# One planned kernel, a new plan: instruction fetches and a slow first clock window booked, sigmoid ordered later, some copies and one scaling in four on VectorE, new urgencies

## The chip, the core and the metric

The kernel runs on one core of a Trainium2 chip. Its metric is the device time in microseconds (us), as the median of several runs. A run's time is that of the whole execution; a profiled execution also has a span, from the first to the last instruction. The engines are PE (TensorE, the matrix engine, with PEld for its weight loads), DVE (VectorE), ACT (ScalarE), POOL (GpSimd) and SP (SyncE, which here only issues DMAs).

## The reference, cut to what matters

The input has 2048 rows of 640 channels, all in float32.

```python
def _A_ref(q, k, v, shift_k, ssm_k, ssm_D):
    k_shift = jnp.zeros_like(k)                     # causal depthwise convolution with 4 taps
    for t in range(ks):
        k_shift = k_shift + k_pad[:, t:t + S, :] * shift_k[:, ks - 1 - t][None, None, :]
    kv = k_shift * v
    y_f = rfft(kv padded to 2S) * rfft(ssm_k padded to 2S)   # per channel
    y = irfft(y_f)[:S] + kv * ssm_D                 # long causal convolution and a skip
    return q * y

def _B_ref(x, w1, b1, w2, b2):
    h = jnp.einsum("bsd,df->bsf", x, w1) + b1
    h = relu(h) ** 2
    return jnp.einsum("bsf,fd->bsd", h, w2) + b2

sa, ca, ga, sb, cb, gb = split(_silu(c) @ w_mod, 6)
h = _layernorm(x) * (1 + ca) + sa                   # x is A_q
x = x + ga * _A_ref(h, A_k, A_v, A_shift_k, A_ssm_k, A_ssm_D)
h = _layernorm(x) * (1 + cb) + sb
x = x + gb * _B_ref(h, B_w1, B_b1, B_w2, B_b2)
```

## The kernel before, in words

**Recording and planning.** The kernel's code does not issue instructions. Each helper adds a node to a graph: an engine, a cost, the tiles it reads and writes, and a key with a number within that key. `Graph.order` (L225) then plans: it runs through a modelled time, and whenever an engine is free it gives it the ready node with the highest urgency for which a buffer is free. The urgency comes from the table `URGE` (L1277; a key's list, one number per node, in tenths), and from the length of the work behind a node where the table has no entry. `emit` (L432) issues all nodes in the planned order, and `keep_order` (L525) pins each engine to that order. So costs and rules of the planner act on the chip only through the order in which each engine's instructions stand, and through the buffers that are given to tiles. All instructions that are issued this way have L439 in the profile (SP's DMAs L632), so they are told apart by tile names.

**What the planner books.** For PE it books the work of a group, an entry and leaving time when the shape of the array's use changes from group to group (`ENTER`, `LEAVE`, L30-31; 64x64, 64x128, 128x128 and so on), a slower clock in windows of 3.4 us after windows with little PE work (`rate`, L229), and one fetch of instructions for every 256 PE instructions (L375-379). DVE instructions with two inputs in SBUF, and all POOL instructions, are booked as exclusive of each other (`lock`). SP has at most six DMAs in flight (`OUT`, L26; the waits are real ones, L631-636), and a DMA may be issued 2 us before its urgency (`HOLD`, `early`, L308).

**First part: the convolution, for 5 blocks of 128 channels.** Per block b: `kv_load` and `kv` (L840, L849) load k and v (tiles named KV), transpose them on PE (`ident,KV`), do the four taps on ACT, DVE and POOL (tiles kacc or KV, with ktail and kover for the three columns that cross a tile's edge), multiply by v, and store the product in DRAM (`kv_d`). `load_h` and `load_x` (L897, L902) load the long filter (`in_A_ssm_k`) and that product into the tile `p`, 4 DMAs each; behind each filter DMA POOL adds the skip `dsm` to the first column (`p<-p,dsm`). `unit_a` (L919) is the first Fourier stage: per block 4 units on the filter and 4 on the product, each of 32 matmuls of 64x64 on PE (`cst,p`), which the trace shows as 64 records, since it shows a float32 matmul twice (and a transpose once). `spectra` (`a,gb`) is the second stage; `front` multiplies the two spectra on DVE and combines them on POOL (tiles wx); `back` (`gi,wx`) and `unit_y` (`ident,q`, then `wx,cst` and `we,cst`) go back to time. In `unit_y` a copy from PSUM to SBUF stands behind each transposition, two per unit (L1026, keys `tc`). `prep` (L1063) normalizes q with four scalings of 128x128 on ACT (L1071, `KV<-xp,nm,rs` and `up<-xp,nm,rs` in the trace), multiplies by a row on DVE and adds a row on POOL; `finish` adds the result to q and stores it (`x_d`). `awake` (L907) adds 20 groups of four transpositions of the unit matrix that nobody reads, to keep PE's clock up; they are booked to the key `warm` and go where the planner puts them.

**Beside it:** `q_stats` takes the statistics of q on DVE, `mod_start` (L740) loads c and takes its sigmoid on ACT, `mod_row` and `mod_col` scale rows of w_mod on ACT by silu(c), add them on POOL (tiles wm) and sum them on PE (`wm,ones`), which gives the rows that `prep` needs. The weights of the MLP are split into two parts on ACT, DVE and POOL (tiles w_S, w_W, w_KA).

**Second part: the MLP, for 8 chunks of 256 rows.** `prep_hat` normalizes, `prep_xt` transposes and splits into two parts (tiles mtmp, xfs, xt), `mlp_front`, `mlp_middle`, `mlp_back` and `mlp_out` follow, with PE matmuls of `xt,w` and of `w,hring`. The table has no entry for most of this part.

Of the kernel before, what the change touches and what calls it, by code (L numbers as in the profile page):

```python
# [13 lines left out]
AF = mybir.ActivationFunctionType  # L14
# [17 lines left out]
ALIKE = 2.0  # L32
ENTER = {(64, 128): 0.104}
# [88 lines left out]
class Graph:  # L122
# [102 lines left out]
    def order(self, lag=0.06, pelag=0.1, phase=0.0):  # L225
# [82 lines left out]
        def early(n):  # L308
            return 1e4 if not n.told else HOLD if n.engine == "SP" else 30.0 if n.key[0] == "warm" else 1e4
# [14 lines left out]
        block, ent = 0.0, 0  # L324
# [6 lines left out]
        while done < len(nodes):  # L331
            moved = False
            for e in ready:
                while free[e] <= t + 1e-9:
# [30 lines left out]
                    if e == "PE":  # L365
# [4 lines left out]
                        last = end = run(t, work)  # L370
# [130 lines left out]
def ssm_mlp_kernel(  # L501
# [153 lines left out]
    def cost(engine, op, args, kw):  # L655
# [7 lines left out]
        if engine == "DVE":  # L663
# [351 lines left out]
    def unit_y(b, l):  # L1015
        ts = []
        qv = QT[b].rearrange("p (n c) k -> p n (c k)", c=2)
        for h in range(2):
# [7 lines left out]
            copy(dve if b == NB - 1 and h else act, s, t)  # L1026
# [36 lines left out]
    def prep(b, j):  # L1063
# [190 lines left out]
    def mlp_out(n):  # L1254
# [18 lines left out]
        if n < NC - 1:  # L1273
# [4 lines left out]
        ("b1", 0): [-1644, -1479],  # L1278
        ("comb", 0): [-476, -465, -479, -469, -486, -532, -539, -490, -546, -553, -560, -582, -600, -614, -607, -640,
            -647, -657, -664],  # L1280
        ("comb", 1): [-952, -962, -966, -945, -995, -955, -988, -1006, -1000, -1024, -1013, -1031, -1053, -1118,
            -1098, -1111, -1105, -1195, -1208],
        ("comb", 2): [-1509, -1547, -1533, -1512, -1551, -1540, -1526, -1561, -1554, -1591, -1590, -1625, -1618,
            -1697, -1690, -1757, -1720, -1767, -1750],
        ("comb", 3): [-1958, -1954, -1937, -1969, -1989, -1982, -1975, -2006, -1999, -2013, -2085, -2066, -2092,
            -2163, -2099, -2157, -2146, -2190, -2183],
        ("comb", 4): [-2392, -2385, -2396, -2403, -2436, -2410, -2429, -2495, -2440, -2476, -2354, -2509, -2502,
# [440 lines left out]
```

## Time and profile before

| | |
|---|---|
| median of 3 runs | 702.28 us (702.1 to 705.56) |
| the profiled execution's own time | 701.26 us |
| its span | 699.5 us |
| what lies around the span | 1.76 us |
| mean granted PE clock | 0.982 |
| PE busy | 653.8 us (93% of the span) |
| DVE, ACT, POOL busy | 398.8, 328.1, 261.4 us |

Times in the trace are counted from the span's start. A row of the timeline has start, length, engine, operation, output and inputs, and in square brackets how long the engine was idle before it and what ended that wait. "issue" means that nothing the profile shows was waited for. In the groups by line, the numbers behind the bar are the busy time in us, the mean length of one instruction in ns, and the idle time before them.

### The profile page before, as it was taken

What the parts mean: (1) busy time and instruction counts of PE and PEld (TensorE: products, weight loads), DVE (VectorE), ACT (ScalarE), POOL (GpSimd) and SP (SyncE); (2) the same over time, 40 slices, a digit from 0 to 9 for tenths busy, and PEclk for the clock granted to TensorE, in tenths of its full rate; (3) what the DMA queues carried; (4) which work ended last, traced back from release to release, by engine and by line L of the source; (5) the groups of instructions that cost most, each with busy time, mean ns of one, the idle gap of its engine ahead of it and who ended that gap; (6) DMA issues with size and microseconds to landing.
All of it is one profiled execution on the core that took longest, in us unless ns stands there. A gap on an engine that the chain in (4) does not pass through costs nothing.

```text
span 699.5 us, 17953 instructions
## 1 busy us (share of the span) xinstructions
PE 653.8 (93%) x7593; PEld 588.6 (84%) x7593; DVE 398.8 (57%) x782; ACT 328.1 (47%) x678; POOL 261.4 (37%) x332
## 2 busy tenths in 40 slices
PE   8859889789889999799999999999999999999996
PEld 8748669658778878499989889999999999999996
DVE  2855846879569367867345474375355463563532
ACT  3626666897777775556323253224233243242220
POOL 2607539969749477444101321004013021030000
PEclk9899999999999999999999999999999999999999
DMA  9797899898954856224002010020020020110011
GB/s 233 211 265 249 220 247 204 246 225 180 244 124 128 169 165 182 87 76 142 0 9 68 19 58 1 1 75 1 1 76 1 9 68 1 30 47 1 1 39 37
DMA packets 108292, 72.42 MB, mean 104 GB/s; under 512 B 48498, under 2 KB 95666, under 8 KB 108212
## 3 DMA queue, kind: packets, MB, share of 16 engines
q1 hardware_dynamic: 106304, 70.80, 39.2%
q8 instruction: 59, 0.97, 0.6%
q10 hardware_dynamic: 1844, 0.48, 0.4%
q14 instruction: 21, 0.17, 0.1%
q0 software_dynamic: 64, 0.01, 0.0%
HBM read 56.85 MB, written 14.42 MB: 102 GB/s over the span
## 4 chain that ended last, share of the span: by engine, by line
PE 83%; DVE 6%; issue 4%; POOL 3%; ACT 2%; DMA 1%; DVEq 0%; SPq 0%; ACTq 0%; POOLq 0%
PE ps L439 83%; DVE KV L439 2%; DMA wm<-in_w_mod_dram 1%; DVE mtmp L439 1%; POOL kover L439 1%; POOL KV L439 1%; ACT a L439 1%; DVE x L439 1%; DVE xt L439 0%; ACT KV L439 0%; DVE up L439 0%; POOL xt L439 0%; ACT wm L439 0%; POOL wm L439 0%; DVE wx L439 0%
## 5 line engine op out<-in xcount | busy, mean ns | idle before, releaser
L439 PE MATMUL ps<-xt,w_S 128*128 128x512 f32 (+1 forms) x935 | 176.8, 332 | 5.4 <-DVE xt L439 2.4
L439 PEld LDWEIGHTS ps<-xt,w_S 128*128 128x128 f32 x935 | 142.2, 190 | 20.4 <-DVE xt L439 2.6
L439 PE MATMUL ps<-w_S,hring 128*128 128x320 f32 x648 | 109.5, 310 | 0.0
L439 ACT ACTIVATE mtmp<-ps,b1t 128x256 f32<-128x256 f32 (+1 forms) x112 | 51.4, 473 | 110.9 <-PE ps L439 102.8
L439 PEld LDWEIGHTS ps<-w_S,hring 128*128 128x128 f32 x648 | 99.0, 188 | 2.1 <-DVE mtmp L439 0.2
L439 DVE TENSOR_TENSOR mtmp<-ps,mtmp 128x256 f32<-128x256 f32 (+1 forms) x99 | 41.0, 420 | 76.8 <-ACT mtmp L439 76.0
L439 PE MATMUL ps<-a,gb 128*64 128x128 f32 x1260 | 80.7, 286 | 1.8 <-ACT a L439 1.0
L439 PEld LDWEIGHTS ps<-a,gb 128*64 128x64 f32 x1260 | 75.0, 144 | 8.0 <-ACT a L439 3.2
L439 DVE TENSOR_TENSOR hring<-mtmp,hring 128x256 fp32r<-128x256 f32 x74 | 39.0, 532 | 50.8 <-ACT hring L439 50.5
L439 PEld LDWEIGHTS ps<-cst,p 64*64 64x64 f32 x2560 | 43.8, 141 | 25.9 <-issue 18.2
L439 PE MATMUL ps<-cst,p 64*64 64x64 f32 x2560 | 49.1, 228 | 17.5 <-issue 12.8
L439 ACT ACTIVATE hring<-mtmp 128x256 fp32r<-128x256 f32 x74 | 30.6, 415 | 73.4 <-PE ps L439 60.0
L439 POOL TENSOR_TENSOR wx<-wx 128x256 f32<-128x256 f32 x80 | 60.0, 771 | 3.9 <-DVE wx L439 3.4
L439 POOL TENSOR_TENSOR x<-x,gb2row 128x640 f32<-128x640 f32 x16 | 25.7, 1625 | 92.0 <-ACT mtmp L439 92.0
L439 POOL TENSOR_TENSOR x<-mtmp,x 128x640 f32<-128x640 f32 (+1 forms) x9 | 13.1, 1461 | 121.9 <-DVE mtmp L439 121.9
L439 ACT ACTIVATE a<-ps 128x512 f32<-128x512 f32 x72 | 41.2, 635 | 35.8 <-PE ps L439 35.7
L439 PE MATMUL ps<-w_S,w_W 128*128 128x320 f32 x312 | 52.7, 308 | 0.0
L439 DVE TENSOR_TENSOR wx<-ps,wx 128x512 f32<-128x512 f32 x64 | 41.2, 685 | 14.9 <-PE ps L439 10.4
L439 PEld LDWEIGHTS ps<-w_S,w_W 128*128 128x128 f32 x312 | 48.3, 188 | 1.2
L439 DVE SCALAR_TENSOR_TENSOR mtmp<-mtmp 128x256 f32<-128x256 f32 x91 | 44.5, 497 | 1.9
L439 PE MATMUL ps<-gi,wx 64*128 64x128 f32 x640 | 40.8, 278 | 3.0 <-issue 1.8
L439 PEld LDWEIGHTS ps<-gi,wx 64*128 64x128 f32 x640 | 37.2, 188 | 6.8 <-issue 4.6
(140 smaller groups left out, 1067.7 us busy)
## 6 DMA issues: line engine op xcount, KB each, us to landing
wm<-in_w_mod_dram SPq DMA_DIRECT2D x25, 320.0 KB, 5.2
KV<-in_A_k_dram SPq DMA_DIRECT2D x20, 256.0 KB, 5.7
p<-in_A_ssm_k_dram SPq DMA_DIRECT2D x20, 256.0 KB, 5.6
KV<-in_A_v_dram SPq DMA_DIRECT2D x20, 256.0 KB, 5.2
p<-kv_d SPq DMA_DIRECT2D x20, 256.0 KB, 5.2
xp<-in_A_q_dram SPq DMA_DIRECT2D x10, 512.0 KB, 8.3
q<-in_A_q_dram SPq DMA_DIRECT2D x7, 640.0 KB, 5.7
out_dram<-x SPq DMA_DIRECT2D x14, 320.0 KB, 3.6
```

The source lines that it names most:

```text
L439: fn(*real, **{k: a.real() if isinstance(a, View) else a for k, a in kw.items()})
```

## The change

Nothing is added to or taken from the computation. There are six edits:

1. The planner books PE's fetches in another way: the first 63 entries of a block of 256 count as already used, a fetch takes 3.6 us, or 5.5 us where a modelled transfer is under way, and a group waits only when PE gets to the next block before its fetch is done.
2. PE's first clock window of 3.4 us is booked as slow.
3. The DMAs that store the output are no longer held back until 2 us before their urgency.
4. The sigmoid is ordered behind the last store of `kv_d` of block 0 in the plan (not by a wait on the chip).
5. In `unit_y` the second copy of each unit is on DVE for blocks 2, 3 and 4 (before: for block 4 only): 8 copies of 128x512 move from ACT to DVE. In `prep` the fourth scaling of each group is a `tensor_scalar` on DVE: 20 of 80 scalings move, and a cost for such an instruction with an input in PSUM is added.
6. All urgencies are other numbers.

```diff
+FETCH = (3.6, 5.5)
@@ rate
                 if k < 4:
-                    slow[k] = False
+                    slow[k] = k == 0
@@ early
-            return 1e4 if not n.told else HOLD if n.engine == "SP" else 30.0 if n.key[0] == "warm" else 1e4
+            return 1e4 if not n.told else HOLD if n.engine == "SP" and n.key[0] != "out" else 30.0 if n.key[0] == "warm" else 1e4
@@ order
-        block, ent = 0.0, 0
+        block, ent = 0.0, 63
...
-                        last = end = run(t, work)
+                        end = run(t, work)
+                        ent += n.entries
+                        if ent >= 256:
+                            ent -= 256
+                            at = end - (end - t) * ent / n.entries
+                            block, late = max(at, block), max(0.0, block - at)
+                            end += late
+                            block += FETCH[dma_free > block]
+                        last = end
...
-                    if e == "PE":
-                        ent += n.entries
-                        if ent >= 256:
-                            end = max(end, block + 4.0)
-                            block, ent = end, ent - 256
@@ cost
+            if op == "tensor_scalar" and deep and len(ins) > 2:
+                return 0.28 + 0.001 * n
@@ mod_start
         act.activation(sg, ct, AF.Sigmoid)
+        g.nodes[-1].deps.add(max(n.id for n in g.nodes if n.key == ("kst", 0)))
@@ unit_y
-            copy(dve if b == NB - 1 and h else act, s, t)
+            copy(dve if b > 1 and h else act, s, t)
@@ prep
-            act.activation(u[:, i], XPt[b][:, l], AF.Identity, scale=rs, bias=nm)
+            if i == 3:
+                dve.tensor_scalar(u[:, i], XPt[b][:, l], rs, nm, op0=ALU.mult, op1=ALU.add)
+            else:
+                act.activation(u[:, i], XPt[b][:, l], AF.Identity, scale=rs, bias=nm)
@@ URGE
-        ("b1", 0): [-1644, -1479],
...
```

The table moves almost every instruction of the first part. Three places show how.

**SP, from the program's first DMA on** (KV are tiles of k and v, `p_0` is block 0's tile for filter and product, `gb` a table of the second Fourier stage, `q_8` rows for the statistics). Before:

```order
L632 DMA KV_87<-in_A_k_dram 128x4x128
L632 DMA p_0_107<-in_A_ssm_k_dram 128x8x64
L632 DMA KV_87<-in_A_v_dram 128x4x128
L632 DMA p_0_107<-in_A_ssm_k_dram 128x8x64
L632 DMA KV_87<-in_A_k_dram 128x4x128
L632 DMA KV_87<-in_A_v_dram 128x4x128
L632 DMA KV_87<-in_A_k_dram 128x4x128
L632 DMA p_0_107<-in_A_ssm_k_dram 128x8x64
L632 DMA KV_87<-in_A_v_dram 128x4x128 x2
L632 DMA KV_87<-in_A_k_dram 128x4x128
L632 DMA gb_270<-in_gb_dram 128x1024
L632 DMA p_0_107<-in_A_ssm_k_dram 128x8x64
```

Of the change:

```order
L637 DMA p_0_106<-in_A_ssm_k_dram 128x8x64
L637 DMA KV_87<-in_A_k_dram 128x4x128
L637 DMA p_0_106<-in_A_ssm_k_dram 128x8x64
L637 DMA KV_87<-in_A_k_dram 128x4x128
L637 DMA p_0_106<-in_A_ssm_k_dram 128x8x64
L637 DMA KV_87<-in_A_v_dram 128x4x128 x2
L637 DMA p_0_106<-in_A_ssm_k_dram 128x8x64
L637 DMA KV_87<-in_A_v_dram 128x4x128
L637 DMA KV_87<-in_A_k_dram 128x4x128
L637 DMA q_8_247<-in_A_q_dram 128x1280
L637 DMA KV_87<-in_A_k_dram 128x4x128
L637 DMA gb_332<-in_gb_dram 128x1024
```

The fourth filter tile moves from the 13th to the 8th DMA; statistics rows come ahead of the last k tile and of gb. On PE, at the same place, 13 of the 20 groups of `awake` now stand ahead of the first unit (before: all 20); the other seven stand singly further on.

**PE, around the last units on block 1's product** (`cst,p_1` is such a unit, `wm_1_0,ones` sums a row of w_mod, `we,cst` and `wx,cst` belong to `unit_y`). Before, two whole units stand on each side of one half of the row's sum:

```order
L439 MATMUL ps3_93<-cst_76,p_1_457 64x64 x2
L439 MATMUL ps2_92<-cst_76,p_1_457 64x64 x2
L439 MATMUL ps3_93<-cst_76,p_1_457 64x64 x2
L439 MATMUL ps6_96<-wm_1_0_1055,ones_70 128x320
L439 MATMUL ps0_90<-cst_76,p_1_457 64x64 x2
L439 MATMUL ps1_91<-cst_76,p_1_457 64x64 x2
L439 MATMUL ps0_90<-cst_76,p_1_457 64x64 x2
```

Of the change, with the sum elsewhere:

```order
L444 MATMUL ps2_92<-cst_76,p_1_390 64x64 x2
L444 MATMUL ps3_93<-cst_76,p_1_390 64x64 x2
L444 MATMUL ps7_97<-we_89,cst_76 64x512
L444 MATMUL ps7_97<-wx_88,cst_76 64x512
L444 MATMUL ps6_96<-ident_63,KV_87 128x128 x4
L444 MATMUL ps5_95<-ident_63,q_0_1070 128x128 x4
L444 MATMUL ps4_94<-ident_63,KV_87 128x128 x4
L444 MATMUL ps2_92<-cst_76,p_1_390 64x64 x2
L444 MATMUL ps3_93<-cst_76,p_1_390 64x64 x2
```

The four units (128 program matmuls) now stand in pieces of 32, 48, 16 and 32 with transpositions and `unit_y` matmuls between them. Counted over the whole PE order, the shape of the array's use changes 120 times before and 132 times in the change; 5 of the 12 more are around single groups of `awake`.

**POOL, where the MLP begins** (`x1_0` and `x1_1` are the first two chunks, `gb2row` a row that is added to them, `xp_4` and `up0` are block 4's results). Before:

```order
L439 TENSOR_TENSOR gb2row_3877<-gb2row_3877,gbrow_4023 128x640
L439 TENSOR_TENSOR xp_4_3352<-xp_4_3352,up0_1190 128x512 x2
L439 TENSOR_TENSOR x1_0_2083<-x1_0_2083,gb2row_3877 128x640
L439 TENSOR_TENSOR xp_4_3352<-xp_4_3352,up0_1190 128x512
L439 TENSOR_TENSOR x1_0_2083<-x1_0_2083,gb2row_3877 128x640
L439 TENSOR_TENSOR mtmp_4075<-mtmp_4075 128x256 x3
```

Of the change:

```order
L444 TENSOR_TENSOR gb2row_3962<-gb2row_3962,gbrow_3977 128x640
L444 TENSOR_TENSOR xp_4_3334<-xp_4_3334,up0_1222 128x512 x2
L444 TENSOR_TENSOR x1_0_2026<-x1_0_2026,gb2row_3962 128x640 x2
L444 TENSOR_TENSOR x1_1_2085<-x1_1_2085,gb2row_3962 128x640
L444 TENSOR_TENSOR xp_4_3334<-xp_4_3334,up0_1222 128x512
L444 TENSOR_TENSOR x1_1_2085<-x1_1_2085,gb2row_3962 128x640
```

The last `xp_4` addition moves out from between the two `x1_0` additions to behind the first `x1_1` addition.

More of the change, by code (lines that the diff above doesn't have):

```diff
@@ new lines, in ssm_mlp_kernel @@
+        ("gate", 0): [-2578, -2550, -2477, -2522, -2586, -2553, -2441, -2518, -2541, -2525, -2665, -2544, -2066,
+            -2040, -2191, -2162, -2757, -2610, -2653, -3144, -3160, -3208, -3035, -2775],
+        ("gb", 0): [-208, -235, -311, -280],
+        ("gi", 0): [-1270, -1263, -1315, -1211],
+        ("h", 1): [-534, -692, -519, -1139, -904, -1044, -1021, -964, -971, -393, -988, -1022, -1044, -1327, -742,
+            -1186],
+        ("h", 2): [-411, -1382, -1398, -1399, -3243, -1563, -1764, -1583, -1533, -1610, -1373, -1635, -1627, -1665,
+            -527, -1705],
@@ new lines, in ssm_mlp_kernel @@
+        ("h", 3): [-554, -1801, -1606, -1808, -3035, -1979, -2203, -1997, -434, -2025, -2182, -1940, -4250, -2115,
+            -1405, -1900],
+        ("h", 4): [-3332, -2315, -2437, -2413, -1874, -2467, -230, -1809, 1621, -2229, -90, -2601, -228, -2405, -250,
+            -3098],
+        ("hat", 0): [-2382, -2788],
+        ("hat", 1): [-2811, -2839],
[25 rows of a table added]
+        ("kst", 0): [-296, 584, -47, -332],
+        ("kst", 1): [987, -567, 1035, 204],
+        ("kst", 2): [-1046, -1140, -1284, -1242],
+        ("kst", 3): [-1282, -1424, -1000, -1147],
@@ new lines, in ssm_mlp_kernel @@
+        ("kst", 4): [-1347, -1835, -1314, -1716],
+        ("kt", 0): [-297, -620, 1686, 124],
+        ("kt", 1): [-72, -491, 1344, -767],
+        ("kt", 2): [-1378, -955, -1274, -1261],
+        ("kt", 3): [-1339, -1370, -1464, -1769],
+        ("kt", 4): [-1503, -2322, -1652, -1379],
+        ("lgb", 0): [-176, -246],
+        ("lgi", 0): [-476, -55, -499],
[35 rows of a table added]
+        ("lxp", 0): [-1077, -764],
+        ("lxp", 1): [-1171, -984],
+        ("lxp", 2): [-1508, -1583],
+        ("lxp", 3): [-1455, 249],
@@ new lines, in ssm_mlp_kernel @@
+        ("mul", 2): [-1540, -1533, -1569, -1548, -1573, -1580, -1590, -1597, -1639, -1760, -1654, -1661, -1717,
+            -1724, -1763, -1756],
+        ("mul", 3): [-1998, -2007, -2014, -2034, -2055, -2041, -2083, -2070, -2090, -2097, -2135, -2128, -2188,
+            -2181, -2196, -2203],
+        ("mul", 4): [-2436, -2437, -2452, -2445, -2470, -2463, -2488, -2481, -2505, -2498, -2542, -2535, -2560,
+            -2554, -2600, -2584],
+        ("out", 0): [-3379, -3410, -3372, -3434, -3425, -3460, -3999, -3991],
[8 rows of a table added]
@@ new lines, in ssm_mlp_kernel @@
+        ("pac", 4): [-2226, -2252, -2258, -2260, -2195, -2203, -2220, -2232, -2423, -2424, -2336, -2342, -2374,
+            -2408, -2396, -2414],
+        ("pra", 0): [-1272, -1160, -1189, -1155, -1174, -1190, -1159, -1152, -687, -1174, -1165, -1133, -1143, -990,
+            -1139, -1128],
+        ("pra", 1): [-1295, -1301, -1278, -1335, -1498, -1528, -1525, -1395, -1420, -1395, -1426, -1384, -1524,
+            -1469, -1301, -1263],
+        ("pra", 2): [-1732, -1958, -1766, -1699, -1716, -1720, -1688, -1686, -1674, -1666, -1672, -1660, -1681,
+            -1625, -1688, -1664],
@@ new lines, in ssm_mlp_kernel @@
+        ("pra", 3): [-2143, -2093, -2085, -2098, -2085, -2132, -2130, -2137, -2103, -2112, -1846, -2114, -2073,
+            -2108, -2119, -2117],
+        ("pra", 4): [-2295, -2327, -2313, -2295, -2301, -2435, -2361, -2292, -2383, -2332, -2369, -2298, -2321,
+            -2357, -2342, -2289],
+        ("prm", 0): [-1315, -1308, -1183, -1158],
+        ("prm", 1): [-1325, -1702, -1435, -1631],
+        ("prm", 2): [-1816, -1740, -1692, -1709],
+        ("prm", 3): [-2255, -2222, -2174, -2215],
@@ new lines, in ssm_mlp_kernel @@
+        ("prm", 4): [-2352, -2425, -2392, -2385],
+        ("prp", 0): [-1418, -1332, -1203, -1190],
+        ("prp", 1): [-1470, -1761, -1498, -1844],
+        ("prp", 2): [-1884, -1944, -1904, -1821],
+        ("prp", 3): [-2350, -2337, -2274, -2281],
+        ("prp", 4): [-2362, -2557, -2375, -2342],
+        ("qp", 0): [-216, -1009, 984, 193],
+        ("qp", 1): [-1094, -1153, -1193, -1267],
+        ("qp", 2): [-992, -1499, -1629, -1918],
+        ("qp", 3): [-1336, -1708, -1168, -795],
+        ("qp", 4): [-2334, -2216, -2218, -2043],
```

129 lines of the change are left out of this document (33 added, 96 removed), and 356 rows, old and new, of the table URGE.

## The prediction

> **What bounds the kernel now.** I read first the page's chain of work that ended last, then the busy time in two windows, cut where the MLP's matmuls begin.
>
> ```profile
> PE 83%; DVE 6%; issue 4%; POOL 3%; ACT 2%; DMA 1%; DVEq 0%; SPq 0%; ACTq 0%; POOLq 0%
> ...
> 0.00:291.00 291.00, 257.23 (x5026) 215.83 (x5026) 190.65 (x325) 193.57 (x372) 180.29 (x251) 0.96 0.80 201
> 291.00:699.50 408.50, 396.56 (x2568) 372.78 (x2567) 208.12 (x458) 134.55 (x306) 81.11 (x82) 0.99 0.12 34
> ```
>
> The columns of a window are its length, busy time (and count) of PE, PEld, DVE, ACT and POOL, granted clock, DMA share and GB/s. PE is the bound, and its work is unchanged. So a new order can only win back PE's idle time: 33.8 us before 291 us, and 11.9 us after it, of which the end of the program takes a part that no order removes. Next, who ended PE's waits, and the queue that carries instructions:
>
> ```profile
> PE ps L439 <- issue: 15.0, 11, 4.0
> ...
> q8 instruction: 59, 0.97, 0.6%
> ```
>
> Nearly half of the early idle time, 15.0 us in 11 waits, waits for nothing that is computed. The queue moved 0.97 MB in 59 packets, 16.4 KB each; PE's 7593 matmuls and as many weight loads make 64 bytes per instruction, so one packet is 257 instructions, or 128 matmuls. The chain in order of time shows that spacing:
>
> ```profile
> 96.56 1.73 issue
> ...
> 230.25 0.67 issue
> 230.92 7.16 PE ps L439 x127
> 238.09 0.26 issue
> 238.35 4.66 PE ps L439 x128
> 243.01 0.32 issue
> 243.33 3.25 PE ps L439 x127
> 246.58 0.85 issue
> ```
>
> Each "issue" wait stands 127 or 128 matmuls behind the last. PE waits when it runs through a block faster than the next is fetched; from wait's end to wait's end is 7.4, 5.0 and 4.1 us. These are the lengths of a fetch here, with other transfers under way in the first and few in the last.
>
> **Term 1, fetches: -1.7 us.** To price a block in the new order I use the mean cost per record of four groups:
>
> ```profile
> L439 PE MATMUL ps<-cst,p 64*64 64x64 f32 x2560 | 49.1, 228 | 17.5 <-issue 12.8 <-POOL p L439 4.3 <-ACT a L439 0.4
> L439 PE MATMUL ps<-a,gb 128*64 128x128 f32 x1260 | 80.7, 286 | 1.8 <-ACT a L439 1.0 <-DVE KV L439 0.8
> L439 PE MATMUL ps<-ident,KV 128*128 128x128 f32 x160 | 24.3, 288 | 3.5 <-DVE KV L439 1.6 <-DVE a L439 0.8 <-DMA KV<-in_A_k_dram 0.4
> ...
> L439 PE MATMUL ps<-wx,cst 128*64 128x512 f32 x40 | 21.3, 614 | 0.0
> ```
>
> They give 0.019, 0.064, 0.152 and 0.53 us (the last for a pair: `we,cst` writes the other 64 partitions beside `wx,cst`). A block of only `cst,p` records runs 2.5 us, shorter than any fetch above. Counted along both orders, the block that ends in the 1.73 us wait at 96.56 ran about 3.2 us by these costs; its successor holds 12 transpositions and four `unit_y` pairs beside 108 records of units, 1.8 + 2.1 + 2.1 = 6.0. That wait goes: -1.7. Of the waits from 230 to 247 (2.1 us together) the two shortest blocks grow from about 4.4 and 3.5 us to 5.4 and 4.7, above the fetches of 5.0 and 4.1; 0.6 us may stay at the long fetch: -1.5. Against that, one block of block 2's filter units shrinks from 5.7 to 3.9, and one of block 4's from 4.4 to 3.2: at a fetch of 4.1 to 5.0 they add about 1.0 and 0.5. The three short blocks of block 0's product units stay (8.4 us of work before, 8.8 now). Bounds: with other work covering the new short blocks -3.2; with a fetch of 7.4 us at both, +4.5.
>
> The Trainium skill, "Runtime: NRT & Kernel Launch", section "Instruction fetch mechanics", says that the sequencer fetches 16 KiB blocks of 256 instructions and that crossing a boundary is "mostly hidden". The block size agrees with 16.4 KB per packet; "hidden" does not agree with 15.0 us here. By that rule this term would be 0, and the sum below 1.7 us higher.
>
> **Term 2, the start: -2.5 us.**
>
> ```profile
> 1.35 10.62 PE L439 MATMUL ps<-ident 128*128 128x128 f32 x80 [1.35 <-POOL ident masks.py:199]
> ...
> 23.39 2.08 PE L439 MATMUL ps<-cst,p 64*64 64x64 f32 x64 [2.51 <-POOL p L439]
> ...
> 8.11 0.37 POOL L439 TENSOR_TENSOR p<-p,dsm 128x8 f32<-128x8 f32 x2
> ```
>
> PE spends 10.62 us on 80 `awake` transpositions, though the first two filter tiles are ready at 8.48 (POOL's row). With 52 of them the units start at about 8.5, 3.4 us sooner, and the moved 28 fill later waits. The fourth filter tile, behind which PE waits 2.51 us before 23.39, goes out as the 8th DMA instead of the 13th. What is late next is the gb table, which now stands behind 640 KB more, and the stores of the kv product. Bounds: 0 if those end the stage as now, -3.4 if nothing does. I take three quarters.
>
> **Term 3, changes of shape: +1.0 us.**
>
> ```profile
> 50.77 0.69 PE L439 MATMUL ps<-cst,p 64*64 64x64 f32 x32 [1.44 <-issue]
> 51.39 0.65 PE L439 MATMUL ps<-ident,KV 128*128 128x128 f32 x4
> ...
> 58.80 1.16 PE L439 MATMUL ps<-cst,p 64*64 64x64 f32 x64
> 59.89 2.84 PE L439 MATMUL ps<-a,gb 128*64 128x128 f32 x48
> ```
>
> From start to next start, 32 records take 0.62 us and 64 take 1.09: 0.0147 each and 0.15 per visit. Twelve more changes cost 1.8 us; the five around single `awake` groups I put into waits, which leaves 1.0. Bounds 0 and 1.8.
>
> **Term 4, work from ACT to DVE: 0.**
>
> ```profile
> 70.00:105.00 35.00, 30.10 (x480) 22.02 (x480) 22.75 (x52) 24.22 (x43) 15.94 (x21) 0.95 0.89 233
> 105.00:140.00 35.00, 31.37 (x638) 27.77 (x634) 25.48 (x40) 26.22 (x55) 31.97 (x46) 1.00 1.01 225
> 140.00:175.00 35.00, 31.21 (x581) 24.84 (x580) 29.61 (x47) 28.41 (x61) 28.17 (x35) 1.00 0.85 202
> ...
> L439 ACT ACTIVATE KV<-xp,nm,rs 128x128 f32<-128x128 f32 x56 | 24.5, 492 | 1.7 <-DVE up L439 1.4 <-POOL xp L439 0.3
> ...
> L439 ACT ACTIVATE wx<-ps 128x512 f32<-128x512 f32 x49 | 29.2, 597 | 15.2 <-PE ps L439 12.9 <-ACT KV L439 1.1 <-ACT up L439 0.8
> ...
> L439 DVE COPY hs<-ps 128x512 f32<-128x512 f32 x4 | 2.7, 686 | 1.3 <-PE ps L439 1.3
> ...
> L439 DVE TENSOR_SCALAR mtmp<-x,rs,nm 128x640 f32<-128x640 f32 x1 | 0.6, 614 | 0.0
> ...
> L439 DVE TENSOR_SCALAR cbs<-ps 128x5 f32<-128x5 f32 x2 | 0.3, 160 | 5.5 <-PE ps L439 5.5
> ```
>
> ACT loses 20 x 0.492 and 8 x 0.597, 14.6 us. DVE gains 8 x 0.686 and 20 scalings of 128x128, which lie between 0.160 (five columns) and 0.614 us (640); I take 0.25, on the straight line between the two: 10.5 us in all, at most 17.8. Two in five scalings belong to blocks 0 and 1, whose stage is 105 to 175 us. There DVE has 55.1 us of 70 busy, ACT 54.6: 2.0 more on DVE fit its gaps, as 3.9 less on ACT opens its own. Bounds -2 and +7 (the rival below).
>
> **Term 5, the MLP's begin: -1.0 us.**
>
> ```profile
> 289.86 1.55 POOL L439 TENSOR_TENSOR x<-x,gb2row 128x640 f32<-128x640 f32 x1 [1.11 <-ACT mtmp L439]
> ...
> 291.37 1.27 POOL L439 TENSOR_TENSOR xp<-xp,up 128x512 f32<-128x512 f32 x1
> 291.46 3.13 DVE L439 TENSOR_TENSOR xt<-xfs,xt 128x256 fp32r<-128x256 f32 x2 [0.46 <-ACT xt L439]
> ...
> 292.60 1.72 POOL L439 TENSOR_TENSOR x<-x,gb2row 128x640 f32<-128x640 f32 x1
> ...
> 294.65 0.57 PE L439 MATMUL ps<-xt,w_S 128*128 128x256 f32 x2 [2.35 <-DVE xt L439]
> ```
>
> Two DVE subtractions with both inputs in SBUF take 3.13 us while POOL adds without a gap until 294.32, and PE waits 2.35 us for them. The order moves the 1.27 us `xp` addition out of that run, so it can end 1.3 sooner, and a bit is lost to the addition that now follows. Bounds -2.4 and +1.
>
> **Term 6, other waits from 70 to 175 us: -1.0.** PE is idle 12.3 us in the three windows above, 10.6 without the 1.73 us fetch, in waits that the fetches do not explain. The new order has the statistics and the w_mod rows earlier, with other waits in their place that the old trace cannot show; I take a tenth off, bounds -4 and +4.
>
> **The sigmoid: 0.** Its table load moves from a time at which ACT had nothing to do to one at which it has little:
>
> ```profile
> 6.24 1.28 ACT L439 ACT_TABLE_LOAD   x1 [1.98 <-DMA cst<-in_cw_dram]
> ...
> 40.00:50.00 10.00, 5.13 (x192) 4.67 (x192) 4.19 (x9) 1.64 (x3) 0.21 (x1) 0.83 1.02 317
> ```
>
> ACT's 8.4 free us there cover it; without them it costs 1.3. Releasing output stores earlier changes nothing while the MLP's stores have no urgencies in the table: 0.
>
> **Sum.** -1.7 - 2.5 + 1.0 - 1.0 - 1.0 = -5.2 us against the profiled execution's 701.26 us, of which 1.76 lie around the span: 696.1. The median of the runs shown is 1.0 above that execution, so I forecast 697.1 us. The measurement of this kernel tells about 0.5% (3.5 us) from no change: faster is below 698.8, slower above 705.8.
>
> **Rivals.** *DVE becomes the bound from 105 to 175 us, slower (chance 0.27).* DVE instructions that use SBUF wait for POOL additions there, as at 291.46, and POOL has 60.1 of 70 us busy. If each of the 8 moved scalings waits for one whole addition (1.27 us) and takes its upper price (0.61), DVE gets 15.0 us, just its 14.9 us of gaps, and most of it would delay the taps and with them PE: +10 to the sum, 707 us. It decides from about half of the scalings waiting. For it: the page's chain runs through DVE and POOL rows in that stage. Against: ACT, the other link, gets freer, and 12 scalings lie later, where PE lost almost nothing to DVE. The Trainium skill, "SBUF — State Buffer", section "Who interferes with whom", states that `tensor_scalar` can take a mode that locks a port pair shared with GpSimd for the whole instruction; the 3.13 us row agrees for subtraction, and no run here shows it for a scaling.
>
> *The early gain is swallowed, no change (0.22).* DMA has 0.89, 1.01 and 0.85 of its time busy in the three windows of term 4. If transfers end each of these stages, terms 2 and 6 are 0: 701.26 - 1.7 + 1.0 - 1.0, plus 1.0, is 700.6 us.
>
> *The fetch booking does not do what it says (0.05).* If fetches on the chip don't follow blocks as booked, term 1 is 0: 698.8 us.
>
> *Far more goes (0.10).* If the plan also removes most of term 6's 10.6 us, 688 us.
>
> **How the numbers follow.** The forecast has 0.36. Faster: 0.36 and 0.10, and half of the 0.05: 0.48. Same: 0.22 and the rest, 0.25. Slower: 0.27. The range reaches over forecast, swallowed gain and the nearer half of the DVE rival: 690 to 707.5 us. The case of faster alone has 693 to 699.
>
> **What would show it.** Term 1: "issue" waits of about 12 to 13 us instead of 15.0, and no such wait among block 1's last units. Term 2: the first `cst,p` record at 8.5 instead of 11.9 us, and no wait for POOL p near 23. Term 3: `cst,p` busy time up by about 1 us. Term 4: scalings on DVE of about 0.25 us; the rival, if they last over 1 us. Term 5: the wait for DVE xt under 1.5 us. The forecast is wrong if PE's idle time before the MLP stays above 32 us.

## The result, and the profile after the change

The changed kernel takes 696.72 us (median of 20 runs, 692.48 to 701.29), the kernel before 702.32 us (median of 20, 697.04 to 710.1). The ratio is 0.9929, 95% interval 0.9905 to 0.9953: faster, by 0.5 to 0.95%. The forecast was 697.1. Its sum was right, half of its terms were not; that their errors cancel was luck.

The profiled execution of the changed kernel took 697.55 us, span 695.7: 3.7 us less than the profiled one of before, where the medians differ by 5.6. First its page's chain and two windows, cut as before just ahead of the MLP's first matmul (now at 287.60):

```profile
PE 83%; DVE 5%; ACT 4%; DMA 3%; issue 3%; POOL 1%; SPq 0%; DVEq 0%; ACTq 0%; POOLq 0%
```

```profile
0.00:286.80 286.80, 255.28 (x5026) 214.13 (x5026) 203.83 (x357) 177.53 (x339) 181.15 (x251) 0.98 0.76 200
286.80:695.70 408.90, 397.62 (x2568) 374.38 (x2567) 205.19 (x455) 137.33 (x311) 80.81 (x82) 0.99 0.13 37
```

PE's idle time before the MLP is 31.5 us instead of 33.8. That is 2.3 us of the gain; PE's busy time is also less, 255.3 instead of 257.2 us, for the same matmuls at a granted clock of 0.98 instead of 0.96. After the cut the time is 0.4 us longer. The largest of PE's waits in the whole profile, grouped by who ended them (total, times, longest; the one for `xt` is the MLP's):

```profile
PE ps L444 <- issue: 12.0, 9, 2.7
PE ps L444 <- ACT a L444: 6.6, 7, 2.4
PE ps L444 <- DVE wx L444: 3.0, 5, 1.2
PE ps L444 <- DVE xt L444: 2.6, 1, 2.6
```

Issue waits fell from 15.0 to 12.0 us. All other waits until the MLP's first matmul rose a little, from 19.2 to 19.9 us; the largest share now waits for ACT's `a`. So in this pair of profiles the gain of 3.8 us of span is 3.0 from fetches and 1.9 of busy time, which goes with the higher clock, less 0.7 in other waits and 0.4 after the MLP began. The timeline of the waits that the steps below speak of:

```profile
9.73 2.10 PE L444 MATMUL ps<-cst,p 64*64 64x64 f32 x128
...
22.92 2.08 PE L444 MATMUL ps<-ident,KV 128*128 128x128 f32 x12 [2.51 <-ACT kacc L444]
...
43.00 5.04 PE L444 MATMUL ps<-cst,p 64*64 64x64 f32 x224 [2.38 <-ACT a L444]
49.90 0.68 PE L444 MATMUL ps<-cst,p 64*64 64x64 f32 x28 [1.86 <-issue]
...
178.17 0.44 PE L444 MATMUL ps<-cst,p 64*64 64x64 f32 x10 [1.80 <-issue]
...
227.84 0.48 PE L444 MATMUL ps<-gi,wx 64*128 64x128 f32 x2 [2.74 <-issue]
```

The units begin at 9.73 instead of 11.90, the long wait for POOL p at 23.39 is gone, and one of the same length for ACT kacc stands at 22.92. No issue wait is left among block 1's last units (94 to 98 us); a new one of 2.74 us stands in block 4.

### The profile page after: what moved, and what is told of

Same layout as the page of the kernel before. It is cut to its first block, busy times and chain, and to the rows that moved or that the text cites. A ratio compares the mean times of both kernels' runs of the same rounds, so it can differ in the third digit from the quotient of the medians.

```text
span 695.7 us, 17972 instructions
## 1 busy us (share of the span) xinstructions
PE 652.9 (94%) x7593; PEld 588.5 (85%) x7593; DVE 409.0 (59%) x810; ACT 314.9 (45%) x650; POOL 262.0 (38%) x332
## 4 chain that ended last, share of the span: by engine, by line
PE 83%; DVE 5%; ACT 4%; DMA 3%; issue 3%; POOL 1%; SPq 0%; DVEq 0%; ACTq 0%; POOLq 0%
PE ps L444 83%; DVE KV L444 2%; ACT a L444 2%; DVE wx L444 1%; DMA p<-in_A_ssm_k_dram 1%; DVE mtmp L444 1%; DMA kv_d<-KV 1%; DMA p<-kv_d 1%; DMA kv_d<-kacc 1%; DVE xt L444 0%; ACT KV L444 0%; ACT q L444 0%; POOL xt L444 0%; ACT wx L444 0%; ACT wm L444 0%
## 5 line engine op out<-in xcount | busy, mean ns | idle before, releaser
L444 ACT ACTIVATE mtmp<-ps,b1t 128x256 f32<-128x256 f32 (+1 forms) x112 | 50.0, 473 | 116.5 <-PE ps L444 112.9
L444 PE MATMUL ps<-a,gb 128*64 128x128 f32 x1260 | 78.5, 279 | 5.4 <-DVE wx L444 2.6
L444 PEld LDWEIGHTS ps<-a,gb 128*64 128x64 f32 x1260 | 71.1, 139 | 13.3 <-DVE wx L444 4.1
L444 DVE TENSOR_TENSOR hring<-mtmp,hring 128x256 fp32r<-128x256 f32 x74 | 37.6, 513 | 54.2 <-ACT hring L444 53.7
L444 PE MATMUL ps<-cst,p 64*64 64x64 f32 x2560 | 51.0, 229 | 13.0 <-issue 7.8
L444 PEld LDWEIGHTS ps<-gi,wx 64*128 64x128 f32 x640 | 38.6, 191 | 8.5 <-issue 6.3
```

Source lines behind the costliest of these rows:

```text
L444: fn(*real, **{k: a.real() if isinstance(a, View) else a for k, a in kw.items()})
```

## Experiments

All of them but the last leave the order of everything else as it was; `plan` in a diff is the planner's order, edited just before it is emitted, and `...` stands for lines left out. Ratios are to the kernel before, run beside them on the same chip; the changed kernel's is 0.9929. One profile is one execution, and profiles of the same order differ by several us, so the verdicts on time rest on the ratios.

**The sigmoid early again.** In the changed kernel ACT loads a table, makes the sigmoid and scales two `wm` tiles just ahead of the copy `a` that PE waits for at 43.00. The chain in order of time:

```profile
39.17 1.28 ACT L444
40.47 0.22 ACT sg L444
40.71 0.18 DVE sg L444
40.91 1.55 ACT wm L444 x2
42.45 0.50 ACT a L444
```

With the dependence of the change taken out again (one of the two scalings goes to the front with the sigmoid, and nothing else changes its place):

```diff
         act.activation(sg, ct, AF.Sigmoid)
-        g.nodes[-1].deps.add(max(n.id for n in g.nodes if n.key == ("kst", 0)))
```

> The changed kernel with the sigmoid ordered early again, everything else in the changed order. In the changed kernel's trace the table load (1.28 us), the sigmoid, its product on DVE and two wm scalings (1.55 us) stand on ACT between 39.17 and 42.45, ahead of the copy a for which PE waits 2.38 us at 43.00. Theory A, the late sigmoid costs PE time: the wait near 43 falls below 1.0 us and most of the 1.9 us comes out at the end, 694.8 to 695.8 us against 696.7. Theory B, the time goes to the next fetch of instructions (its wait of 1.86 us at 49.90 grows by what the wait at 43 loses): 696.2 to 697.2 us.

Measured: 699.77 us, ratio 0.9954 (0.9928 to 0.9980). Not faster, so theory A falls. The time is above what theory B allows too, by the ratios 0.25% above the changed kernel, with intervals that overlap. The timeline shows theory B's exchange of waits:

```profile
39.55 1.67 PE L444 MATMUL ps<-cst,p 64*64 64x64 f32 x97 [0.80 <-ACT a L444]
41.74 1.66 PE L444 MATMUL ps<-cst,p 64*64 64x64 f32 x95 [0.52 <-issue]
43.55 0.69 PE L444 MATMUL ps<-cst,p 64*64 64x64 f32 x32 [0.15 <-ACT a L444]
48.47 0.69 PE L444 MATMUL ps<-cst,p 64*64 64x64 f32 x28 [4.22 <-issue]
```

The wait for `a` shrinks from 2.38 to 0.95 us and the fetch behind it grows from 1.86 to 4.74. Both stand over blocks that hold little but `cst,p` records; there the fetch is the limit, and ACT's work is hidden as long as it ends before the fetch.

**The scalings and copies on ACT again.**

```diff
+    for _, _, n in plan:
+        fn, op, args, kw = n.calls[0]
+        if n.key[0] == "pra" and n.engine == "DVE":
+            n.calls = [(nc.scalar.activation, op, (*args[:2], AF.Identity), dict(scale=args[2], bias=args[3]))]
+        if n.key[0] == "tc" and n.key[1] in (2, 3) and n.engine == "DVE":
+            n.calls = [(nc.scalar.activation, op, (*args[:2], AF.Copy), {})]
```

> The changed kernel in its own order, with the 20 scalings and the 8 copies that the change gave to DVE issued on ACT again. Theory A, the prediction's term 4: both engines have gaps, the time stays within 1 us of 696.7. Theory B, the moves are what the change lives from: PE waits for ACT already in the changed trace (6.6 us for a, 2.5 for kacc, 1.7 for q), and 14.6 us more on ACT lengthen those waits: 699 us or more. Theory C, DVE is late in the changed kernel: 16.6 us less on it give 694.7 us or less.

Measured: 697.01 us, ratio 0.9924 (0.9891 to 0.9957): theory A. The part of the change that moves work between engines is worth nothing that the interval of some 2 us could show, either way.

**All awake transpositions first.**

```diff
+    plan.sort(key=lambda o: o[2].key[0] != "warm")
```

> The changed kernel with all 80 awake transpositions before the first unit, as in the kernel before, everything else in the changed order. Theory A, the prediction's term 2: the units start 3.4 us later and most of it stays, 699.2 us. Theory B, the trace: the early start was lost again by 40 us to waits for kacc and a, so that it is worth nothing: 696.2 to 697.7 us, and the PE wait of 2.51 us for kacc near 23 is shorter by what the start is later.

Measured: 700.60 us, ratio 0.9996 (0.9971 to 1.0020). Theory B, which I had read from the two timelines, falls: without this step the whole gain of the change is gone. Theory A is right in kind; the loss by the ratios is 0.67%, 4.7 us, against the 2.5 expected.

**The same step alone, on the kernel before.** 28 transpositions are moved ahead of the fourth filter unit.

```diff
+    warm = [o for o in plan if o[2].key[0] == "warm"][13:]
+    plan = [o for o in plan if o not in warm]
+    at = [i for i, o in enumerate(plan) if o[2].key == ("pa", 0) and o[2].engine == "PE"][6]
+    plan[at:at] = warm
```

> The kernel before, with 28 of its 80 awake transpositions moved from the front to just ahead of the fourth filter unit, where PE waits 2.51 us for POOL p at 23.39; the order of DMAs and all else is the kernel before. Theory A, the transpositions at the front are what the start costs: the units begin 3.4 us sooner and 2.5 to 4.7 us of that stay, 697.6 to 699.8 us against 702.3. Theory B, the fourth filter tile's DMA (13th of its queue) ends the start, and only the changed kernel's order of DMAs makes room for an earlier start: 701.3 to 703.3 us, with the fourth unit at 23.4 us or later.

Measured: 696.91 us, ratio 0.9898 (0.9854 to 0.9943). In this kernel the moved transpositions overwrite a PSUM bank that holds transposed v, so its output is another. With them in a free bank:

```diff
+    ...
+    for o in warm:
+        g.place[o[2].bufs[0].n] = 0
```

> The kernel before, with 28 of its 80 awake transpositions moved from the front to just ahead of the fourth filter unit, all into one PSUM bank that is free there; the order of DMAs and all else is the kernel before. (In the first such kernel the moved transpositions overwrote a bank with transposed v, so that its output was another; its median was 1.0% under the kernel before.) Theory A, the transpositions at the front are what the start costs: 697 to 699.8 us against 702.3, ratio 0.990 to 0.9965. Theory B, only the changed order of DMAs makes room for an earlier start, and the first such run was chance: ratio 0.9985 to 1.0015.

Measured: 693.34 us, ratio 0.9878 (0.9834 to 0.9921). Theory A holds, and by more than it expected: this one step gives as much as the whole change or more. The timeline shows the start, and windows of 5 us the clock (the number ahead of the last two), of the kernel before first and then with the step:

```profile
1.35 7.42 PE L439 MATMUL ps<-ident 128*128 128x128 f32 x52 [1.35 <-POOL ident masks.py:199]
8.70 1.63 PE L439 MATMUL ps<-cst,p 64*64 64x64 f32 x96
...
18.06 3.22 PE L439 MATMUL ps<-ident 128*128 128x128 f32 x28
21.21 0.91 PE L439 MATMUL ps<-cst,p 64*64 64x64 f32 x44
```

```profile
20.00:25.00 5.00, 2.26 (x62) 2.03 (x66) 4.86 (x10) 3.88 (x5) 4.59 (x10) 0.69 0.35 120
25.00:30.00 5.00, 4.97 (x62) 4.45 (x56) 4.11 (x8) 3.45 (x8) 3.73 (x9) 0.63 0.69 202
```

```profile
20.00:25.00 5.00, 4.39 (x96) 3.73 (x96) 4.71 (x10) 3.98 (x8) 3.26 (x6) 1.00 0.53 187
25.00:30.00 5.00, 5.00 (x96) 4.94 (x94) 4.85 (x10) 3.37 (x6) 2.11 (x7) 1.00 0.69 175
```

The units start 3.2 us sooner, and the transpositions keep PE busy where it had waited 2.51 us. Before, that wait was followed by a clock of 0.63 to 0.69; now it is 1.00. In the changed kernel the same windows have 0.87 and 0.79, with all 80 first again 0.73 and 0.66.

**Without the 28 transpositions.**

```diff
+    ...
+    plan = [o for o in plan if o not in warm]
+    for _ in range(14):
+        nc.tensor.matmul(bank[7][0:1, 0:1], ones[:, 0:1], ones[:, 0:1], start=True, stop=True)
```

> The changed kernel without the 28 awake transpositions that it places between the units of the start, with 14 matmuls of one column at the very front in their place, so that the block boundaries after them stay where they are. Theory A, they stand in waits of PE: within 1 us of the changed kernel, ratio 0.9915 to 0.9945. Theory B, they cost PE time and changes of shape (3.7 us of work, seven groups): 1.5 to 3.5 us faster, ratio 0.988 to 0.991. Theory C, they hold the clock up: without them the clock is lower from 15 to 45 us and the kernel is slower, ratio over 0.9955.

Measured: 697.91 us, ratio 0.9936 (0.9910 to 0.9963): theory A in time, and theory C in the clock, which falls to its half where the transpositions are missing:

```profile
20.00:25.00 5.00, 2.94 (x40) 2.09 (x39) 3.25 (x7) 3.79 (x8) 1.30 (x4) 0.50 0.65 194
25.00:30.00 5.00, 4.72 (x29) 4.09 (x30) 4.59 (x10) 1.90 (x2) 2.70 (x3) 0.50 0.47 124
```

PE has some 3.7 us less to do and does the rest more slowly: its busy time is 653.2 us where the changed kernel's is 652.9.

**The MLP's begin.** In the changed kernel POOL (first row) still adds beside DVE's two subtractions (second row), and PE waits:

```profile
285.66 4.71 POOL L444 TENSOR_TENSOR x<-x,gb2row 128x640 f32<-128x640 f32 x3 [1.12 <-ACT mtmp L444]
...
287.27 3.39 DVE L444 TENSOR_TENSOR xt<-xfs,xt 128x256 fp32r<-128x256 f32 x2
...
290.71 1.65 PE L444 MATMUL ps<-xt,w_S 128*128 128x256 f32 x6 [2.61 <-DVE xt L444]
```

The experiment holds the four additions back until the last of the first tile's subtractions; `behind` and `noted` add that dependence.

```diff
+    late = [o for o in plan if o[2].key[0] == "f2" and o[2].engine == "POOL" and o[0] < 310]
+    ...
+    late[0][2].calls = [behind(c) for c in late[0][2].calls]
+    at = xt[-1] + 1
+    plan[at:at] = late
```

> The changed kernel with the four POOL additions of gb2row to x (4.71 us in a row from 285.66, and 1.66 us) held back until the last DVE subtraction of xt of the first tile; nothing else is moved. Theory A, DVE waits for POOL's additions and the clock falls after PE's wait: the pair of subtractions takes 0.9 us instead of 3.39, PE's wait of 2.61 us for it goes, and with it most of the half clock from 290 to 296.6 us: 691.5 to 693.5 us against 696.7. Theory B, contention alone (the clock is half there whatever the wait): 694 to 694.7 us. Theory C, the subtractions are slow for another reason: 696.7 us, 3.4 us for the pair.

Measured: 696.62 us, ratio 0.9912 (0.9879 to 0.9944), and 405.1 us from the MLP's first matmul to the end. That part is 408.1 us in the changed kernel's profile, and 406.8 to 408.1, mean 407.2, in the six profiles of the changed order whose kernels leave it alone. By the ratios the time is not clearly under the changed kernel's. The DVE row, then the two waits of PE left there:

```profile
286.45 0.76 DVE L1718 TENSOR_TENSOR xt<-xfs,xt 128x256 fp32r<-128x256 f32 x2 [0.19 <-ACT xt L444]
```

```profile
286.77 9.15 PE L444 MATMUL ps<-xt,w_S 128*128 128x256 f32 x72 [0.71 <-ACT xt L444]
300.11 2.05 PE L444 MATMUL ps<-w_S,w_W 128*128 128x320 f32 x11 [1.75 <-ACT w_W L444]
```

The pair takes 0.76 us instead of 3.39, so POOL's additions were what held it. Theory A's mechanism is shown; its size is not reached, since POOL now adds until 297.8 and its first products are late, for which ACT's `w_W`, and with it PE, waits at 300. So the additions go where POOL has a gap:

```diff
+    ...
+    at = [i for i, o in enumerate(plan) if o[2].key == ("mid", 0) and o[2].engine == "POOL"][10] + 1
+    plan[at:at] = late
```

> The changed kernel with the four POOL additions of gb2row to x moved behind POOL's eleventh product of the first tile's MLP (near 328 us, where POOL stands idle for 7.8 us). Holding them back until the subtractions of xt had freed PE of 2.61 us and of the half clock, but PE then waited 1.75 us at 300 us for products that stood behind the additions; from the first matmul of the MLP to the end the span was 405.1 us against 408.1. Theory A, both waits go: 403.0 to 404.0 us for that part and 691.7 to 692.9 us in all. Theory B, the additions now hold up the DVE subtractions at 328 to 335 us and PE with them: 405 us or more for that part, 694 us or more in all.

Measured: 691.78 us, ratio 0.9814 (0.9766 to 0.9862), and 403.1 us for the part from the MLP's first matmul on: theory A. This version beats both kernels, the changed one by 1.1% of the ratios, or 8 us. Its MLP explains 4 to 5 of them; the rest lies within the intervals.

**The wait or the clock?** The next kernel leaves POOL and DVE as they are and fills PE's wait.

```diff
+    first = next(n for _, _, n in plan if n.key == ("f1", 0) and n.engine == "PE")
+    first.calls[2:2] = [(nc.tensor.transpose, "", (bank[0][:, 0:P], ident, ident), {})] * 18
```

> The changed kernel with 18 transpositions of the identity that nobody reads (about 2.4 us of PE work) ahead of the first matmul that waits for DVE xt; the DVE pair still takes about 3.4 us beside POOL's additions. Theory A, the clock is halved because PE stood idle: the granted clock stays at 0.9 or more over the first 8 us of the MLP, and the part from the first matmul of the MLP to the end is 404.8 to 405.6 us instead of 408.1; in all 693.4 to 694.5 us. Theory B, the low clock comes with the MLP's first matmuls whatever ran before: clock 0.5 for 4 to 6 us as in the changed kernel, 408 us for that part and 696.7 in all.

Measured: 694.68 us, ratio 0.9875 (0.9828 to 0.9922), 405.5 us for that part. Two windows behind the wait, of the changed kernel and of this one (the matmul that waits starts at 290.71 and at 288.39):

```profile
290.00:292.00 2.00, 1.29 (x6) 1.29 (x7) 1.41 (x3) 0.66 (x3) 1.79 (x2) 0.50 0.00 0
292.00:294.00 2.00, 2.00 (x11) 2.00 (x11) 1.74 (x4) 1.29 (x3) 1.05 (x1) 0.50 0.04 8
```

```profile
290.00:292.00 2.00, 2.00 (x19) 2.00 (x18) 1.84 (x3) 0.98 (x2) 1.36 (x1) 1.00 0.00 0
292.00:294.00 2.00, 2.00 (x19) 1.92 (x18) 0.59 (x1) 0.64 (x2) 0.31 (x1) 1.00 0.00 0
```

PE does 11 records in 2 us at half clock and 19 at full. Theory A: the idle PE is what lowers the clock. The other profiles agree (the old booking's, with an order of its own, left aside): in all nine whose kernels keep this wait, of 2.34 to 2.63 us, the clock falls to its half for 3.4 or 6.8 us there, and in none of the four in which PE doesn't stand idle for it. The matmul behind the wait starts no sooner, and still 2.6 us go against the changed kernel's profile and 1.7 against the mean of 407.2; that is the part of the price that is paid after the wait.

**Both, and the start's waits filled.** Four matmuls of 256 columns stand ahead of each of the waits for `kacc` and `a`, with POOL's additions in its gap.

```diff
+    ...
+    vt.calls[0:0] = [wide(0)] * 4
+    pa.calls[0:0] = [wide(4)] * 4
```

> The changed kernel with POOL's four additions moved to 328 us (ratio 0.9814 by itself) and four wide matmuls that nobody reads (256 columns, about 2.2 us together, 16 instructions) ahead of each of PE's two long waits of the start, for kacc near 23 us (2.5 us) and for a near 42 us (2.4 to 3.4 us). Theory A, these waits also lower the clock (0.79 to 0.87 from 20 to 30 us, 0.66 to 0.92 from 40 to 55 us in the changed trace): the clock stays at 0.95 or more there and 1 to 3 us go, 689 to 691 us, ratio 0.977 to 0.980. Theory B, the time goes to the fetches and waits for data that follow: the clock is up and the ratio stays at 0.980 to 0.983. Theory C, the added matmuls last longer than the waits: slower, ratio over 0.983.

Measured: 693.98 us, ratio 0.9888 (0.9850 to 0.9926): by its bound theory C, and surely no gain over the 0.9814 without the fill. The first 60 us, of the kernel without the fill and then with it:

```profile
0.00:60.00 60.00, 48.41 (x1054) 43.35 (x1054) 35.35 (x71) 29.52 (x50) 26.48 (x54) 0.94 0.91 243
```

```profile
0.00:60.00 60.00, 50.90 (x1070) 45.10 (x1070) 34.81 (x70) 29.52 (x50) 27.05 (x56) 0.97 0.93 246
```

The clock rose from 0.94 to 0.97, and yet both have done 1054 records of the work by 60 us, since 16 of the 1070 are the fill's. The issue waits of the whole profile are 12.1 us against 7.8. At the start PE only comes to the next fetch sooner; at the MLP's begin, where a block of 128 records lasts some 16 us (72 of them 9.15 us, above) and no issue wait stands, a higher clock counts in full. That the fetches took the gain is argued from one profile each, and why the fill should cost time is open.

**Blocks moved by a half.** 128 PE instructions ahead of everything.

```diff
+    for _ in range(32):
+        nc.tensor.matmul(bank[7][0:1, 0:1], ones[:, 0:1], ones[:, 0:1], start=True, stop=True)
```

> The changed kernel with 32 matmuls of one column before everything else (128 PE instructions, half a block of a fetch, less than 1.5 us); the order is the same, only the boundaries of the instruction blocks move by 64 matmul records. Theory A, the issue waits are fetches that a short block doesn't cover: the waits of the changed kernel near 178 us (1.4 to 1.8 us) and after block 3's filter units go, and new ones come where a whole block now holds cst,p records alone or nearly so (block 3's product units, near 195 us, 1.5 to 3 us; block 4's units, 220 to 230 us, 1.5 to 3 us); in all 696 to 699 us. Theory B, the issue waits belong to the instructions behind them, not to the blocks: they stay at the same matmuls as in the changed kernel, later by the start.

Measured: 701.98 us, ratio 0.9976 (0.9941 to 1.0011). Its issue waits after 170 us:

```profile
201.60 0.69 PE L444 MATMUL ps<-cst,p 64*64 64x64 f32 x32 [1.91 <-issue]
229.10 0.74 PE L444 MATMUL ps<-cst,p 64*64 64x64 f32 x34 [2.12 <-issue]
234.55 0.33 PE L444 MATMUL ps<-cst,p 64*64 64x64 f32 x3 [1.65 <-issue]
```

The wait that stood at 178.17 is gone, and new ones follow the blocks that now hold little but `cst,p` records: theory A, the waits belong to the blocks. The time is above the 696 to 699 us that I expected, by the ratios 3.3 us above the changed kernel, with nearly the same issue waits (12.3 us); why it is that much is open.

**The old booking of fetches.** Here the planner orders anew.

```diff
-block, ent = 0.0, 63
+block, ent = 0.0, 0
...
+                    if e == "PE":
+                        ent += n.entries
+                        if ent >= 256:
+                            end = max(end, block + 4.0)
+                            block, ent = end, ent - 256
```

> The changed kernel with the fetches of instructions booked as before (4.0 us after the last boundary, counted from zero, one length for all); the planner orders anew with it, so PE's order differs from about the 520th matmul on. Theory A, the booking is what lowered the issue waits from 15.0 us in both traces of the old order to 7.8 to 14.7 (mean 9.8) in the seven of the changed one: issue waits of 13 us or more, and 3 to 5 us longer than the changed kernel, ratio to the kernel before 0.997 to 1.001. Theory B, the urgencies carry the order and the booking decides little: issue waits of 8 to 12 us, ratio 0.990 to 0.996.

Measured: 749.69 us, ratio 1.069 (1.0639 to 1.0741). Its issue waits are 15.2 us, as theory A had them, but that explains 3 of the 53 us:

```profile
PE ps L441 <- issue: 15.2, 10, 4.7
PE ps L441 <- DVE wx L441: 12.1, 9, 5.0
PE ps L441 <- ACT a L441: 8.5, 10, 3.6
PE ps L441 <- DVE KV L441: 8.0, 3, 4.2
```

With another model of time the same table of urgencies gives a far worse order, and waits for data grow. This run doesn't tell what the booking is worth.

## Why the prediction was right, and where it was not

**Term 1, fetches (-1.7): right in kind, too small.** The pair shows -3.0. Nine profiles with the changed order (the changed kernel and the eight experiments that leave its order, and its blocks but for 28 records at most) have 7.8 to 14.7 us of issue waits, mean 9.9; three of the old order have 15.0, 15.0 and 11.8. So it is about -4, with a spread of several us. Three parts were mis-sized. The three short blocks of block 0's product units, which I let stay, went from 7.2 us of issue waits (36.87 to 50.77) to 2.9, partly because PE waits for `a` there instead. And the short block among block 4's filter units, priced at +0.5, costs 2.74 in the changed kernel and 2.5 to 4.4 in all nine. From the block's first record to the wait's end are 6.3 us, where I had read fetches of 4.1 to 5.0 a little later in the old trace; the block ahead of it is short too (3.7 us), and whether this fetch was long or began late is open. Thirdly, the term left waits out: those of the old order that end at 190.24 and 197.63 (3.7 us) went, and new ones that end at 73.79, 130.09 and 178.17 (4.1 us) came. The wait at 96.56 and the four from 230 to 247 went as said.

**Term 2, the start (-2.5): the step that carries the change, at half its price.** Undone it costs 4.7 us by the ratios (give or take 2.5), done alone it gives 8.6 (5.5 to 11.7). I counted the 3.4 us by which the units were to start sooner and left out the clock. (They start 3.2 us sooner with this step alone, and 2.2 in the changed kernel's profile: the 52 transpositions take 8.44 us there, 7.3 to 8.4 in the others.) The runs of the kernel before have a mean granted clock of 0.979, those with this step alone 0.987; 0.8% of 653 busy us is 5.2 us, and with the 3.2 us of the earlier start that would make 8.4, an estimate. In the changed order the clock's part isn't separated: without the 28 transpositions the mean clock is 0.978, as with all 80 first, and the time is still 0.6% less. "What is late next" was neither the gb table nor a store but `kacc`.

**Term 3, changes of shape (+1.0): not shown, and miscounted.** By the matmuls in the two traces the shape changes 125 times before and 132 times after, so seven more and not twelve; beside the five around single `awake` groups two are left, 0.3 us at the term's own price. `cst,p` is busy 51.0 us instead of 49.1 in the pair, but 49.3 to 51.7 in the other runs. Without the 28 transpositions and their seven groups the time is the same.

**Term 4, ACT to DVE (0): right,** by the copies and scalings put back. The unit price was wrong: 0.25 us expected, and by the groups of DVE:

```profile
L444 DVE TENSOR_SCALAR KV<-xp,rs,nm 128x128 f32<-128x128 f32 x14 | 7.1, 542 | 0.2 <-DMA xp<-in_A_q_dram 0.2
L444 DVE TENSOR_SCALAR up<-xp,rs,nm 128x128 f32<-128x128 f32 x6 | 4.0, 698 | 3.2 <-DMA xp<-in_A_q_dram 3.2
```

By tile, their shortest, median and longest are 332, 354 and 1301 ns for the first and 333, 458 and 1306 for the second. The long ones stand beside POOL additions (the one of 1.30 us at 129.98 beside an addition from 129.54 to 131.20). So a few do wait for about a POOL addition, as the slower rival had it; too few to hold PE.

**Term 5, the MLP's begin (-1.0): failed.** PE's wait went from 2.35 to 2.61 us. I took it that one addition less in POOL's run would end it sooner; three additions of `x` now stand in a row from 285.66, so the pair is held as long as before. The contention was read rightly, but to thin out the run isn't to leave it: all four additions moved to the gap give 4 to 5 us after the MLP's first matmul, about two fifths of it by the clock (the 1.7 us of the filled wait).

**Term 6, other waits (-1.0): too small there, and given back elsewhere.** From 70 to 175 us PE is idle 10.5 us, 3.6 of it for issue, where it was 12.3 with 1.7:

```profile
70.00:105.00 35.00, 30.91 (x570) 24.72 (x570) 22.81 (x50) 27.06 (x47) 20.72 (x27) 1.00 0.97 262
105.00:140.00 35.00, 31.04 (x654) 27.31 (x654) 31.11 (x48) 27.02 (x57) 28.31 (x39) 1.00 1.00 239
140.00:175.00 35.00, 32.52 (x684) 27.37 (x674) 30.01 (x48) 25.02 (x51) 26.51 (x35) 1.00 0.87 222
```

That is -3.7 in waits that aren't fetches. Ahead of 62 us such waits grew by 2.1 and from 175 us to the MLP by 2.4, so in all they are 0.7 up. The DMA rival, an early gain that is swallowed, is thus true of the waits and not of the time, because it left the clock out as I did. That transfers swallow it isn't shown: none of PE's waits from 70 us to the MLP is put down to a DMA.

**The sigmoid (0): right for another reason.** It doesn't lie in ACT's free time but on PE's path at 43 us, and by the exchange of waits shown above the fetch behind it hides it.

The forecast of 697.1 was met by luck: a start priced too low stood against a block 4 and an MLP's begin priced too well. PE's idle time before the MLP, 31.5 us, passed the forecast's own sign of 32 by little. Everything but the start's step adds up to nothing: 0.9996 with that step undone, and the step alone does no worse than the whole.

## What to carry to other kernels

Price a wait of TensorE with what follows it: where the granted clock falls behind a wait, useless matmuls placed in it are worth a part of its removal (1.7 of some 4 us here), as long as no fetch of instructions is the next limit. Work that only fills belongs in waits, not ahead of the first real work; here the 28 transpositions could as well have been left out (0.9936). When a run of instructions on one engine slows another engine's (3.39 us for the pair instead of 0.76), move the whole run to a gap; and when single executions spread by 1%, take no term of 2 us from one pair of profiles.

## What the hardware showed beyond that

A wait of PE of 2.5 us, with shorter ones beside it, can halve the clock for the next 3 to 6 us: 2.51 us at 23.39 in the kernel before (0.63 to 0.69 over 10 us), 2.61 us at the MLP's begin in the changed one (0.50 from 290 to 296). The Trainium skill, "TensorE: Matmul & The Clock Gate", Part 1, states that the half rate comes after at least one idle window of about 3.4 us, and that the windows run freely, wherever the kernel starts. The traces agree with the second: the same wait of 2.51 us for `kacc` left the clock at 1.00 from 20 to 30 us in two profiles (the sigmoid early; POOL's additions in the gap) and at 0.79 to 0.87 in the changed kernel's. With the first they don't, since a gap well under 3.4 us was enough.

Runs of one kernel spread by about 9 us (the changed one 692.5 to 701.3) and go with their mean granted clock (0.978 to 0.988 over its 20 runs): on a straight line through them 0.01 of clock is 6.7 us. Issue waits in nearly the same blocks differ from profile to profile between 7.8 and 14.7 us.
